# A residual add moved from VectorE to an accumulating DMA in a seven-product Strassen-like cross network kernel

## The chip, the cores and the metric

The kernel runs on one core of one Trainium2 chip. The metric is device time in microseconds (us); most executions agree within 0.3%. TensorE is called PE below, VectorE DVE, ScalarE ACT, GpSimd POOL, and SyncE (which issues most DMAs here) SP.

## The reference, cut to what matters

```python
# x0: [16384, 1024] bf16, ws: [6, 1024, 1024] bf16, bs: [6, 1024] bf16
x = x0
for l in range(6):
    proj = einsum('bd,de->be', x, ws[l]) + bs[l]
    x = x0 * proj + x          # the residual add is the "+ x"
return x
```

## The kernel before

The batch is cut into 16 pairs of 2 x 512 rows. For each pair the transposed input `x0T` and the running `x` (`xst`) lie in SBUF. The 1024 x 1024 product of a layer is done with seven products of half size instead of eight (Strassen-Winograd): each is 16 matmuls of 128x128 on 128x512. `xst` has four blocks, named (eh, n): eh is the half of the features, n the half of the rows. T1 to T4 are differences of blocks, made on DVE, and are inputs of products. The order of the products is 1, 5, 3, 2, 6, 7, 4. Cuts are marked with `# ...`.

```python
rhs_of = {1: blk(xsrc, 0, 0), 2: blk(xsrc, 1, 0), 3: blk(xsrc, 1, 1), 4: Ts[4][:],
          5: Ts[1][:], 6: Ts[2][:], 7: Ts[3][:]}
# T1 = B(0,1) - B(0,0);  T2 = B(1,1) - T1;  T3 = B(1,1) - B(0,1);  T4 = B(1,0) - T2

def final(Cb, eh, n):
    c = Cb[:, :, n, :]
    nc.vector.tensor_tensor(out=c, in0=c, in1=blk(x0T, eh, n), op=MULT)        # L214
    # ... (last layer of the last pair cut)
    nc.vector.tensor_tensor(out=blk(xst, eh, n), in0=c, in1=blk(xsrc, eh, n), op=ADD)   # L223

product(1, pA, True);  P1s = evac(pA)
product(5, pX, True);  P5s = evac(pX)
product(3, pX, False); S53 = evac(pX, bias_eh=0)
product(2, pX2, True); P2s = evac(pX2, bias_eh=0)
nc.vector.tensor_tensor(out=C1[:, :, 0, :], in0=P1s, in1=P2s, op=ADD);  final(C1, 0, 0)
product(6, pA, False)
# ... U2s + S53
final(C1, 0, 1)
# T1 of the next layer
product(7, pA, False)
# ... U3s + P5s
final(C2, 1, 1)
product(4, pA, False)
# ...
final(C2, 1, 0)
# T2, T3, T4 of the next layer
```

Two more things share the DMA engines. Every product loads its own 512 KB of weights, about nine products ahead, all issued in order by SP. At the turn from one pair to the next, SP also issues a transpose of the finished `xst`, two stores of 1 MB, and two transposing loads of the next `x0`.

```python
            if l == (2 if pr == 0 else 0) and not last_pair:
                x0T_next = x0t_pool.tile([P, 2, KD, NB], BF16, name="x0T")
                for n in range(2):
                    ti = nc.sync.dma_start_transpose(out=x0T_next[:, n], in_=x0[...])   # L268
```

Of the kernel before, what the change touches and what calls it, by code (L numbers as in the profile page):

```python
# [7 lines left out]
ADD = mybir.AluOpType.add  # L8
SUB = mybir.AluOpType.subtract
MULT = mybir.AluOpType.mult  # L10
BF16 = mybir.dt.bfloat16
# [5 lines left out]
def kernel(  # L17
# [7 lines left out]
    nc = tc.nc  # L25
    P = nc.NUM_PARTITIONS
# [3 lines left out]
    KH = KD // 2  # L30
    H = D // 2
    NB = 512
# [11 lines left out]
    cb_pool = ctx.enter_context(tc.tile_pool(name="cbp", bufs=2))  # L44
# [29 lines left out]
    def prefetch_upto(n):  # L74
        while state["next"] < min(n, len(all_keys)):
            k_ = all_keys[state["next"]]
            if is_dma(k_) and k_ not in wtiles:
                wt = wring.tile([P, KH, H], BF16, name="wp")
                state["last_dma"] = nc.sync.dma_start(wt[:], w_src(k_[1], k_[2]))
                wtiles[k_] = wt  # L80
            state["next"] += 1

    def blk(t, dh, n):
        return t[:, n, dh * KH:(dh + 1) * KH, :]
# [28 lines left out]
    def load_w12(l):  # L113
        st = combo_st.setdefault(l, {})
        if "w12" not in st:
            st["w12"] = w12_pool.tile([P, KH, H], BF16, name="w12")
            state["last_dma"] = nc.sync.dma_start(st["w12"][:], ws[l][0:H, H:D].rearrange("(k p) e -> p k e", p=P))
        return st["w12"]
# [40 lines left out]
    for pr in range(NPAIR):  # L159
        x0T = x0T_next  # L160
        xst = xst_pool.tile([P, 2, KD, NB], BF16, name="xst")
# [3 lines left out]
        def out_region(eh, n):  # L165
            if xo_last["t"] is None:
                xo_last["t"] = xo_pool.tile([P, 2, 2, KH, KH, P], BF16, name="xoS")
            ti = nc.sync.dma_start_transpose(out=xo_last["t"][:, eh, n].rearrange("p j k r -> p (j k) r"),
                                             in_=xo_last["xfin"][:, eh, n].rearrange("r j k p -> r (j k p)"))
            xo_last["regions"].append((eh, n))  # L170
            xo_last["tins"] = xo_last.get("tins", []) + [ti]
        for l in range(L):
            xsrc = x0T if l == 0 else xst
            Ts = Tn["T"]
            Tn = {"T": {}, "do": ()}
            rhs_of = {1: blk(xsrc, 0, 0), 2: blk(xsrc, 1, 0), 3: blk(xsrc, 1, 1), 4: Ts[4][:], 5: Ts[1][:], 6: Ts[2][:], 7: Ts[3][:]}
            bias_col = lambda eh, m: b_all[:, l * KD + eh * KH + m: l * KD + eh * KH + m + 1]
            if pr == 0 and l + 1 < L:
                prefetch_upto(key_pos[(0, l + 1, 4)] + 1)
                load_w12(l + 1)  # L180
            flush_saves()
            pA = [psA.tile([P, 2, NB], FP32, name="pa") for _ in range(2)]
            C1 = cb_pool.tile([P, KH, 2, NB], BF16, name="cb")
            C2 = cb_pool.tile([P, KH, 2, NB], BF16, name="cb")
            nxt_src = xst if l + 1 < L else None
            combos_next = pr == 0 and l + 1 < L

            def product(pid, pts, start):
                key = (pr, l, pid)
                prefetch_upto(key_pos[key] + PREF)  # L190
                wt = wtiles.pop(key) if not (pr == 0 and pid in (1, 2, 4)) else wtiles[key]
                rhs = rhs_of[pid]
                for m in range(KH):
                    for k in range(KH):
                        kw = {} if start else dict(skip_group_check=True)
                        nc.tensor.matmul(pts[m // 2][:, m % 2, :], lhsT=wt[:, k, m * P:(m + 1) * P], rhs=rhs[:, k, :],  # L196
                                         start=(start and k == 0), stop=(k == KH - 1), **kw)

            def evac(pts, bias_eh=None, dst=None):
                if dst is None:  # L200
                    e = ev_pool.tile([P, KH, NB], BF16, name="ev")
                    dst = e[:]
                if bias_eh is None:
                    for h in range(2):
                        nc.scalar.copy(out=dst[:, 2 * h:2 * h + 2, :], in_=pts[h][:])  # L205
                else:
                    for m in range(KH):
                        nc.scalar.activation(out=dst[:, m, :], in_=pts[m // 2][:, m % 2, :], func=IDENT,  # L208
                                             bias=bias_col(bias_eh, m), scale=1.0)
                return dst  # L210

            def final(Cb, eh, n):
                c = Cb[:, :, n, :]
                nc.vector.tensor_tensor(out=c, in0=c, in1=blk(x0T, eh, n), op=MULT)  # L214
                if last_pair and l == L - 1:
                    if xo_last["xfin"] is None:
                        xo_last["xfin"] = xst_pool.tile([P, 2, 2, KH, KH, P], BF16, name="xst")
                    v4 = lambda a: a.rearrange("r k (j p) -> r k j p", p=P)
                    nc.vector.tensor_tensor(out=xo_last["xfin"][:, eh, n].rearrange("r j k p -> r k j p"),  # L219
                                            in0=v4(c), in1=v4(blk(xsrc, eh, n)), op=ADD)  # L220
                    out_region(eh, n)
                else:
                    nc.vector.tensor_tensor(out=blk(xst, eh, n), in0=c, in1=blk(xsrc, eh, n), op=ADD)  # L223

            product(1, pA, True)
            P1s = evac(pA)
            pX = [psX.tile([P, 2, NB], FP32, name="px") for _ in range(2)]
            product(5, pX, True)
            P5s = evac(pX)
            product(3, pX, False)  # L230
            S53 = evac(pX, bias_eh=0)
            pX2 = [psX.tile([P, 2, NB], FP32, name="px") for _ in range(2)]
            product(2, pX2, True)
            P2s = evac(pX2, bias_eh=0)
            nc.vector.tensor_tensor(out=C1[:, :, 0, :], in0=P1s, in1=P2s, op=ADD)  # L235
            final(C1, 0, 0)
            if combos_next:
                emit_combo(l + 1, 5)
            product(6, pA, False)
            U2s = evac(pA)  # L240
            nc.vector.tensor_tensor(out=C1[:, :, 1, :], in0=U2s, in1=S53, op=ADD)  # L241
            final(C1, 0, 1)
            if nxt_src is not None:
                Tn["do"] = (1,)
                emit_T(nxt_src, Tn)
            if combos_next:
                emit_combo(l + 1, 6)
            product(7, pA, False)
            U3s = evac(pA, bias_eh=1)
            nc.vector.tensor_tensor(out=C2[:, :, 1, :], in0=U3s, in1=P5s, op=ADD)  # L250
            final(C2, 1, 1)
            if combos_next:
                emit_combo(l + 1, 3)
            product(4, pA, False)
            evac(pA, bias_eh=1, dst=C2[:, :, 0, :])
            final(C2, 1, 0)
            if nxt_src is not None:
                Tn["do"] = (2, 3, 4)
                emit_T(nxt_src, Tn)
            if combos_next:  # L260
                emit_combo(l + 1, 7)
                if l + 1 == L - 1:
                    stage_ctx.close()
                    xo_pool = ctx.enter_context(tc.tile_pool(name="xo", bufs=1))
# [3 lines that stand above are left out]
                    ti = nc.sync.dma_start_transpose(out=x0T_next[:, n], in_=x0[(pr + 1) * PR + n * NB:(pr + 1) * PR + (n + 1) * NB, :])  # L268
                    if state.get("last_dma") is not None:
                        tc.add_manual_dep(ti.ins, state["last_dma"].ins.name,  # L270
                                          mybir.DependencyInfo(mybir.DependencyClass.NoSync, mybir.DependencyReason.DATA),
                                          reason="keep the x0 prefetch behind the already issued weight loads")
            if l == L - 1 and not last_pair:
                Tn["do"] = (1, 2, 3, 4)
                emit_T(x0T_next, Tn)
# [47 lines left out]
```

## Time and profile before

| | before |
|---|---|
| time, median of 2 runs | 2353.77 us (2353.34 to 2354.19) |
| PE busy | 2312.4 us, 98% of the span |
| DVE busy | 1708.6 us, 73% |
| the 316 residual adds that the change replaces | 385.0 us of DVE, 1222 ns each |

From the page of the kernel before: the engines' busy times, the chain of waits that ended last, the group of the residual add (count, then busy us and mean ns of one, then idle time before it) and two kinds of DMA (count, KB, median us from issue to landing; for transposes no size).

```profile
span 2352.8 us, 27562 instructions
...
PE 2312.4 (98%) x10537; PEld 1052.7 (45%) x10752; DVE 1708.6 (73%) x1464; ACT 1556.7 (66%) x2113; POOL 1.2 (0%) x5
...
PE 96%; DVE 1%; DMA 1%; issue 1%; SPq 1%; ACT 0%; another core or an unknown queue 0%; DVEq 0%
...
L223 DVE TENSOR_TENSOR xst<-cb,xst 128x2048 bf16<-128x2048 bf16 x316 | 385.0, 1222 | 14.5
...
wp<-Lc SPq DMA_DIRECT2D x360, 512.0 KB, 3.4
...
x0T<-in_x_dram SPq DMA_TRANSPOSE x32, 7.3
```

The chain is PE from end to end, so nothing that DVE does is paid for, as long as it is done in time. How much time there is shows in the timeline of one change of layer (start in us, duration, engine, line, operation). Product 6 of the old layer ended near 1000 us.

```profile
1003.38 1.23 DVE L214 TENSOR_TENSOR cb<-cb,x0T 128x2048 bf16<-128x2048 bf16 x1
1004.64 1.22 DVE L223 TENSOR_TENSOR xst<-cb,xst 128x2048 bf16<-128x2048 bf16 x1
...
1006.92 1.22 DVE L93 TENSOR_TENSOR T_7568<-xst 128x2048 bf16<-128x2048 bf16 x1
1007.25 3.62 PE L196 MATMUL pa<-xst,wp 128*128 128x512 bf16 x15
...
1010.71 3.62 PE L196 MATMUL px<-T_7568,wp 128*128 128x512 bf16 x16
...
1014.16 7.07 PE L196 MATMUL px<-xst,wp 128*128 128x512 bf16 x31
```

These are the multiply and the add of block (0,1), then T1, then products 1, 5, and 3 with 2 of the next layer. A product starts every 3.45 us, and no line has a wait. Three products lie between the end of product 6 and product 5 of the next layer, which needs T1. The add is finished 3.6 us before T1 has to start (1010.71 - 1.22 - 1005.86), so the way from the multiply to T1 has some slack, but not much.

The third thing to read is how full the DMA engines are. The windows view gives, for one layer with the transposing loads of `x0` in it and one plain layer, the busy time of each engine, the granted PE clock, the DMA share (1.00 is all 16 engines) and GB/s:

```profile
1055.90:1080.00 24.10, 24.00 (x112) 10.86 (x113) 17.43 (x16) 16.13 (x23) 0.00 (x0) 1.00 1.08 253
1104.30:1128.40 24.10, 23.94 (x111) 10.90 (x112) 17.50 (x16) 16.13 (x23) 0.00 (x0) 1.00 0.45 153
```

A plain layer leaves half the DMA time free; the layer after the turn leaves none.

### The profile page before, as it was taken

What the parts mean: (1) busy time and instruction counts of PE and PEld (TensorE: products, weight loads), DVE (VectorE), ACT (ScalarE), POOL (GpSimd) and SP (SyncE); (2) the same over time, 40 slices, a digit from 0 to 9 for tenths busy, and PEclk for the clock granted to TensorE, in tenths of its full rate; (3) what the DMA queues carried; (4) which work ended last, traced back from release to release, by engine and by line L of the source; (5) the groups of instructions that cost most, each with busy time, mean ns of one, the idle gap of its engine ahead of it and who ended that gap; (6) DMA issues with size and microseconds to landing.
All of it is one profiled execution on the core that took longest, in us unless ns stands there. A gap on an engine that the chain in (4) does not pass through costs nothing.

```text
span 2352.8 us, 27562 instructions
## 1 busy us (share of the span) xinstructions
PE 2312.4 (98%) x10537; PEld 1052.7 (45%) x10752; DVE 1708.6 (73%) x1464; ACT 1556.7 (66%) x2113; POOL 1.2 (0%) x5
## 2 busy tenths in 40 slices
PE   7999999999999999999999999999999999999997
PEld 3444444444444444444444444444444444444443
DVE  5977767676777767676776767677776767777675
ACT  4666666666666666666666666666666666666665
POOL 0000000000000000000000000000000000000000
PEclk9999999999999999999999999999999999999998
DMA  7769485584956849568494774947749476594843
GB/s 226 203 210 256 152 216 196 161 253 154 228 184 171 241 154 240 171 177 235 153 259 153 178 233 152 259 152 190 221 152 260 153 198 214 155 257 152 226 153 86
DMA packets 599987, 457.96 MB, mean 195 GB/s; under 512 B 398128, under 2 KB 550704, under 8 KB 599856
## 3 DMA queue, kind: packets, MB, share of 16 engines
q1 hardware_dynamic: 599856, 456.20, 67.0%
q8 instruction: 85, 1.39, 0.2%
q14 instruction: 46, 0.38, 0.1%
HBM read 342.88 MB, written 46.14 MB: 165 GB/s over the span
## 4 chain that ended last, share of the span: by engine, by line
PE 96%; DVE 1%; DMA 1%; issue 1%; SPq 1%; ACT 0%; another core or an unknown queue 0%; DVEq 0%
PE pa L196 54%; PE px L196 42%; SPq L145 1%; DMA w_313<-in_ws_dram 0%; DMA wp<-in_ws_dram 0%; DVE cb L214 0%; DVE xst L219 0%; DVE xst L223 0%; ACT ev L208 0%; DVE cb L241 0%; DVE cb L250 0%; DVE cb L235 0%; DVE wp L128 0%; DVE T_247 L93 0%; DVE T_811 L93 0%
## 5 line engine op out<-in xcount | busy, mean ns | idle before, releaser
L196 PEld LDWEIGHTS <-wp 128*128 128x128 bf16 x10752 | 1052.7, 98 | 1283.8 <-issue 12.7
L208 ACT ACTIVATE ev<-px,b_all 128x512 bf16<-128x512 f32 x768 | 486.3, 684 | 201.3 <-PE px L196 193.3
L196 PE MATMUL px<-xst,wp 128*128 128x512 bf16 x2510 | 562.5, 379 | 2.7
L235 DVE TENSOR_TENSOR cb<-ev 128x2048 bf16<-128x2048 bf16 x96 | 117.6, 1225 | 594.2 <-ACT ev L208 594.2
L205 ACT CAST ev<-pa 128x1024 bf16<-128x1024 f32 x384 | 388.6, 1012 | 240.2 <-PE pa L196 230.8
L214 DVE TENSOR_TENSOR cb<-cb,x0T 128x2048 bf16<-128x2048 bf16 x384 | 467.8, 1221 | 6.3
L223 DVE TENSOR_TENSOR xst<-cb,xst 128x2048 bf16<-128x2048 bf16 x316 | 385.0, 1222 | 14.5
L208 ACT ACTIVATE ev<-pa,b_all 128x512 bf16<-128x512 f32 x384 | 243.1, 684 | 112.9 <-PE pa L196 108.2
L208 ACT ACTIVATE cb<-pa,b_all 128x512 bf16<-128x512 f32 x384 | 243.1, 684 | 88.4 <-ACT ev L208 48.4
L196 PE MATMUL pa<-xst,wp 128*128 128x512 bf16 x1254 | 287.3, 379 | 1.3
L205 ACT CAST ev<-px 128x1024 bf16<-128x1024 f32 x192 | 194.3, 1012 | 138.1 <-PE px L196 133.1
L241 DVE TENSOR_TENSOR cb<-ev 128x2048 bf16<-128x2048 bf16 x96 | 117.0, 1219 | 0.0
L250 DVE TENSOR_TENSOR cb<-ev 128x2048 bf16<-128x2048 bf16 x96 | 117.0, 1218 | 0.0
L196 PE MATMUL px<-x0T,wp 128*128 128x512 bf16 x501 | 112.4, 379 | 0.5
L223 DVE TENSOR_TENSOR xst<-cb,x0T 128x2048 bf16<-128x2048 bf16 x64 | 78.3, 1223 | 1.5
L196 PE MATMUL pa<-x0T,wp 128*128 128x512 bf16 x251 | 60.2, 391 | 12.9 <-DMA x0T<-in_x_dram 12.6
L130 DVE TENSOR_TENSOR wp<-wp 128x2048 bf16<-128x2048 bf16 x6 | 7.3, 1219 | 2.1 <-DMA wp<-in_ws_dram 2.1
L128 DVE TENSOR_TENSOR wp<-wp 128x2048 bf16<-128x2048 bf16 x6 | 7.3, 1219 | 0.0
L126 DVE TENSOR_TENSOR wp<-w_90,wp 128x2048 bf16<-128x2048 bf16 x1 | 1.2, 1226 | 8.2 <-DMA wp<-in_ws_dram 8.2
L93 DVE TENSOR_TENSOR T_111<-x0T 128x2048 bf16<-128x2048 bf16 x1 | 1.2, 1226 | 5.7 <-DMA x0T<-in_x_dram 5.7
L219 DVE TENSOR_TENSOR xst<-cb,xst 128x2048 bf16<-128x2048 bf16 x4 | 4.9, 1225 | 0.1
L196 PE MATMUL px<-T_247,wp 128*128 128x512 bf16 x16 | 3.6, 378 | 0.3 <-DVE T_247 L93 0.3
(783 smaller groups left out, 1858.9 us busy)
## 6 DMA issues: line engine op xcount, KB each, us to landing
wp<-Lc SPq DMA_DIRECT2D x360, 512.0 KB, 3.4
wp<-in_ws_dram SPq DMA_DIRECT2D x288, 512.0 KB, 3.7
out_dram<-x0T SPq DMA_DIRECT2D x30, 1024.0 KB, 9.8
Lc<-wp SPq DMA_DIRECT2D x24, 512.0 KB, 3.1
out_dram<-xoS SPq DMA_DIRECT2D x4, 512.0 KB, 4.7
w_90<-in_ws_dram SPq DMA_DIRECT2D x1, 512.0 KB, 4.7
x0T<-in_x_dram SPq DMA_TRANSPOSE x32, 7.3
w_130<-in_ws_dram SPq DMA_DIRECT2D x1, 512.0 KB, 5.0
```

The source lines that it names most:

```text
L128: nc.vector.tensor_tensor(out=t_[:], in0=wtiles[(0, l, 5)][:], in1=W11[:], op=SUB)
L130: nc.vector.tensor_tensor(out=t_[:], in0=W21[:], in1=wtiles[(0, l, 6)][:], op=SUB)
L145: nc.sync.dma_start_transpose(out=x0T_next[:, n], in_=x0[n * NB:(n + 1) * NB, :])
L196: nc.tensor.matmul(pts[m // 2][:, m % 2, :], lhsT=wt[:, k, m * P:(m + 1) * P], rhs=rhs[:, k, :], start=(start and k == 0), stop=(k == KH - ...
L205: nc.scalar.copy(out=dst[:, 2 * h:2 * h + 2, :], in_=pts[h][:])
L208: nc.scalar.activation(out=dst[:, m, :], in_=pts[m // 2][:, m % 2, :], func=IDENT, bias=bias_col(bias_eh, m), scale=1.0)
L214: nc.vector.tensor_tensor(out=c, in0=c, in1=blk(x0T, eh, n), op=MULT)
L219: nc.vector.tensor_tensor(out=xo_last["xfin"][:, eh, n].rearrange("r j k p -> r k j p"), in0=v4(c), in1=v4(blk(xsrc, eh, n)), op=ADD)
L223: nc.vector.tensor_tensor(out=blk(xst, eh, n), in0=c, in1=blk(xsrc, eh, n), op=ADD)
L235: nc.vector.tensor_tensor(out=C1[:, :, 0, :], in0=P1s, in1=P2s, op=ADD)
L241: nc.vector.tensor_tensor(out=C1[:, :, 1, :], in0=U2s, in1=S53, op=ADD)
L250: nc.vector.tensor_tensor(out=C2[:, :, 1, :], in0=U3s, in1=P5s, op=ADD)
```

## The change

The intent: DVE is busy 73% of the time, DMA engines have time to spare, and a DMA issued from GpSimd can add to its destination. So from layer 1 on the residual add `x += x0*proj` becomes an accumulating DMA from the product tile into `xst`. The product tile also gets a layout in which each block is contiguous, for 4 KB rows. Layer 0 keeps the DVE add, since its source is `x0T` and not `xst`.

```diff
-            C1 = cb_pool.tile([P, KH, 2, NB], BF16, name="cb")
-            C2 = cb_pool.tile([P, KH, 2, NB], BF16, name="cb")
+            C1 = cb_pool.tile([P, 2, KH, NB], BF16, name="cb")
+            C2 = cb_pool.tile([P, 2, KH, NB], BF16, name="cb")
 ...
-                c = Cb[:, :, n, :]
+                c = Cb[:, n]
 ...
+                elif l > 0:
+                    nc.gpsimd.dma_start(blk(xst, eh, n), c, accum_op=ADD)
                 else:
                     nc.vector.tensor_tensor(out=blk(xst, eh, n), in0=c, in1=blk(xsrc, eh, n), op=ADD)
 ... (four more lines index C1 and C2 in the new layout)
```

## The prediction

> **What bounds the kernel now.** TensorE. The page gives PE 2312.4 us busy of a 2352.8 us span (98%), the chain of waits is 96% PE, and the granted clock is 1.00 in every layer I read. The timeline shows one product of 16 matmuls starting every 3.45 us and a layer of seven products every 24.17 us. VectorE is busy 1708.6 us (73%), but the waits view shows PE waiting for it only 0.3 us twice.
>
> **Removed.** 316 VectorE adds (group xst<-cb,xst, 1222 ns each): 386 us of VectorE time, none of it on the chain.
>
> **Added.** 316 accumulating DMAs of 512 KB, SBUF to SBUF, issued by GpSimd. Packets of 4096 bytes take 159 ns here, so a plain 512 KB copy keeps each engine busy 8 x 159 ns = 1.27 us. The Trainium skill ("Collectives: The Full Stack", "The bandwidth ceiling") says that a reduce in the DMA needs two source reads and runs at half the copy rate: estimate 2.5 us of data. The fixed part is about 2 us ("DMA: Bandwidth & Descriptors", "Anatomy of one DMA", and the weight loads agree: 3.4 us to landing for 1.3 to 1.6 us of data). Weight loads share the engines, one per 3.45 us (DMA share 0.47 in plain layers, 1.08 in the layer with the x0 transposes). Estimate from the end of the multiply to landing: D = 6.5 us in plain layers, 5 at best, 8 to 10 where transposes and a backlog of weight loads are in the queue. An add took 1.2 us.
>
> **What lies on the critical path.** I read the slack from the timeline at 1000 to 1018 us, times from the end of product 6 (about 1000):
> - (0,0): multiply ends 1000.9, product 1 of the next layer starts 1007.25. Stall if D > 6.4.
> - (0,1): its multiply can end at 4.05; T1 takes 1.22 and product 5 starts at 10.7. Stall D - 5.4.
> - (1,0): VectorE is in order and T1 precedes this multiply, so T1's wait for the DMA holds it. It ends at 6.5 + D and lands at 6.5 + 2D; product 2 was due at 17.6. The accumulated stall is 2D - 11.1.
> - (1,1): never binding.
>
> These stalls recur at 4 layer ends per pair (layers 1 to 4) x 16 pairs = 64. D = 5.5 costs nothing; 6.5 gives 1.9 us x 64 = 122 us; 8 gives 314 us. A gain is nearly impossible.
>
> **Predicted time.** 2490 us, range 2352 to 2760. Faster by over 2%: 0.01; within 2%: 0.24; slower: 0.75.
>
> **What the profile would show.**
> - VectorE busy falls by about 386 us to about 1320 us, with more idle time, ended by the DMA xst<-cb before T1.
> - PE idle appears before product 5 (px<-T1) and product 2 (px<-xst), waiting for VectorE T1 and the DMA; l = 1 is worst.
> - A software queue of 316 DMAs, 166 MB written, median D of 5 to 8 us; DMA share of plain layers rises from 0.47 to about 0.9.
> - Products still start every 3.45 us between stalls; layer 0 of each pair keeps 24.17 us.
>
> **What would make it wrong.** If descriptor generation on GpSimd for a two-source DMA is slow, or the adder in the DMA runs well below half the copy rate, D reaches 10 us and the loss 500 us or more. If contention is milder and D stays under 5.5 us, the time is the same. If a backlog of weight loads starves PE, stalls show on wp, not on xst.

## The result, and the profile after

The changed kernel takes 2753.44 us (median of 2 runs, 2748.07 to 2758.80), against 2353.77 us: 400 us more. The ratio is 1.1698 (95% interval 1.1644 to 1.1753). Ratios here are the mean time of one kernel's runs over that of the other's runs of the same rounds, so not quite the ratio of the medians quoted. The result is correct. The direction was predicted, and the time lies just inside the range, but the loss is three times the 136 us forecast.

The same parts of the page, after:

```profile
span 2746.2 us, 28149 instructions
...
PE 2415.0 (88%) x10752; PEld 1064.7 (39%) x10752; DVE 1369.6 (50%) x1148; ACT 1555.5 (57%) x2113; POOL 273.0 (10%) x321
...
q1 hardware_dynamic: 599856, 456.20, 58.1%
q0 software_dynamic: 45504, 165.70, 33.3%
...
PE 12%; DMA 6%; DVE 2%; ACT 1%; issue 1%; POOL 0%; DVEq 0%; POOLq 0%; ACTq 0%
...
wp<-Lc SPq DMA_DIRECT2D x360, 512.0 KB, 6.4
xst<-cb POOLq DMA_DIRECT2D x316, 512.0 KB, 7.6
...
x0T<-in_x_dram SPq DMA_TRANSPOSE x32, 11.5
```

DVE lost its work (1708.6 to 1369.6 us). The new queue q0 moves 165.70 MB. The accumulating DMA takes 7.6 us from issue to landing where the add took 1.2, and everything else in the DMA queues takes longer too: a weight load 6.4 us instead of 3.4, an `x0` transpose 11.5 instead of 7.3. (The chain of waits accounts for too little of this span to be read.)

**A plain change of layer.** The timeline, for the same steps as shown of before; in brackets the idle time of the engine before the line, and what ended it:

```profile
1164.63 1.22 DVE L214 TENSOR_TENSOR cb<-cb,x0T 128x2048 bf16<-128x2048 bf16 x1
...
1166.15 0.86 POOL L223 DMA_DIRECT2D xst<-cb  x1 [2.11 <-DVE cb L214]
...
1169.03 3.62 PE L196 MATMUL pa<-xst,wp 128*128 128x512 bf16 x16
...
1173.37 1.23 DVE L93 TENSOR_TENSOR T_7387<-xst 128x2048 bf16<-128x2048 bf16 x1 [3.81 <-DMA xst<-cb]
1174.51 1.22 DVE L214 TENSOR_TENSOR cb<-cb,x0T 128x2048 bf16<-128x2048 bf16 x1
1174.65 3.61 PE L196 MATMUL px<-T_7387,wp 128*128 128x512 bf16 x16 [2.00 <-DVE T_7387 L93]
```

The multiply of (0,1) ends at 1165.85 (1164.63 + 1.22), T1 can start at 1173.37: 7.5 us, and product 5 waits 2.0 us. Note the line at 1174.51: the multiply of block (1,0) runs behind T1, although the last ACT operation on its tile had ended at 1170.49.

**The crowded change of layer**, from layer 1 to 2 of a pair, where the `x0` transposes are in the queue:

```profile
1092.44 14.06 SPq L270 DMA_TRANSPOSE x0T<-in_x_dram  x2
...
1099.15 1.23 DVE L214 TENSOR_TENSOR cb<-cb,x0T 128x2048 bf16<-128x2048 bf16 x1
...
1100.67 0.87 POOL L223 DMA_DIRECT2D xst<-cb  x1 [2.09 <-DVE cb L214]
...
1115.98 1.23 DVE L93 TENSOR_TENSOR T_7025<-xst 128x2048 bf16<-128x2048 bf16 x1 [11.90 <-DMA xst<-cb]
...
1117.26 6.35 PE L196 MATMUL px<-T_7025,wp 128*128 128x512 bf16 x16 [9.43 <-DVE T_7025 L93]
```

Here the same step took 15.6 us (1115.98 - 1100.38), product 5 waited 9.4 us, and then its 16 matmuls took 6.35 us instead of 3.6, because the clock had fallen: the trace's clock records show half clock for 10.2 us, from 5.4 us after the gap began.

**Where the 393.4 us of the profiled spans went.** In every trace all 10752 weight loads of PE are recorded. From their start times one gets the idle gap before each product (last weight load of one product to the second of the next, less two matmul pitches of 0.216 us). Summed over the run, in us; the kernel before has 0.9 us in all:

| entry into layer | before product 1 | 5 | 3 | 2 | sum | per entry (16) |
|---|---|---|---|---|---|---|
| 2 | 33.0 | 91.7 | 0.6 | 21.9 | 147.2 | 9.2 |
| 3 | 24.7 | 47.2 | 0.9 | 12.9 | 85.7 | 5.4 |
| 4 | 1.8 | 38.8 | 2.4 | 1.8 | 44.7 | 2.8 |
| 5 | 2.5 | 41.7 | 0.8 | 0.0 | 45.0 | 2.8 |
| all | 62.0 | 219.4 | 4.7 | 36.6 | 322.6 | |

The total with 0.5 us elsewhere is 323 us, 322 more than before. The other 71 us (393.4 - 322) are matmuls at a lower clock. In the trace every one of the 24 products that started after a gap of over 3.5 us was slow (over 1 us longer than 3.45), 12 of the 40 after a gap of 2 to 3.5 us, and of the 608 after a smaller gap only the very first. The Trainium skill says why ("TensorE: Matmul & The Clock Gate", "What's actually happening"): PE falls to half clock after an idle window of about 3.4 us and needs about as much work to come back. The trace agrees in that the recorded clock is 1 or one half and nothing else, and that 22 of its 37 half-clock stretches last 3.4 us and 8 last 6.8. The length of the gap alone does not decide, though: here gaps from 2.2 us on could be enough, and in `e_x0split_t1late`, an experiment below, 7 of the 15 products after gaps of over 3.5 us ran at full clock, the longest of these gaps being 3.84 us.

**What the time of the DMA is made of.** From the records of the DMA packets one can tell when the first packet of each accumulating DMA started and the last ended. D is from the end of the multiply to the end of the last packet; T1, the reader, started another 0.4 to 0.5 us later in the last three runs of the table (layer 4) and 0.6 to 0.8 us later in the change (medians). Medians for block (0,1), pairs 1 to 14:

| run, layer | multiply to issue | issue to first packet | first to last packet | D |
|---|---|---|---|---|
| change, layer 4 | 0.30 | 3.10 | 4.13 | 7.50 |
| change, layer 1 | 0.30 | 6.13 | 5.36 | 10.49 (mean 13.17) |
| `e_copy` (no adding), layer 4 | 0.30 | 2.69 | 1.96 | 4.96 |
| `e_noload` (no weight loads), layer 4 | 0.30 | 1.43 | 2.77 | 4.49 |
| `e_01only` (no other block by DMA), layer 4 | 0.29 | 1.86 | 3.36 | 5.46 |

The last three are experiments below.

What the DMA of (0,1) waits for in a plain layer is not what one might think. In layers 3 and 4 of pairs 1 to 14 its first packet starts, in 25 of 28 cases, 0.5 to 1.6 us after the last packet of (0,0) has ended, and in between the packets of a weight load take 69 to 98% of the engines' time. That weight load is itself held up by (0,0): its first packet comes 1.8 us after its issue and its last 5.0 us, against 1.0 and 3.1 us in the kernel before and 1.1 and 3.0 us in `e_01only` (medians). So in a plain layer the DMAs of the two queues take turns almost as wholes. Without weight loads (`e_noload`) the DMA of (0,0) is there too, and (0,1) doesn't wait for it: 1.43 us from issue to first packet, the same as for (0,0).

### The profile page after: what moved, and what is told of

Same layout as the page of the kernel before. It is cut to its first block, busy times and chain, and to the rows that moved or that the text cites. A ratio compares the mean times of both kernels' runs of the same rounds, so it can differ in the third digit from the quotient of the medians.

```text
span 2746.2 us, 28149 instructions
## 1 busy us (share of the span) xinstructions
PE 2415.0 (88%) x10752; PEld 1064.7 (39%) x10752; DVE 1369.6 (50%) x1148; ACT 1555.5 (57%) x2113; POOL 273.0 (10%) x321
## 3 DMA queue, kind: packets, MB, share of 16 engines
q0 software_dynamic: 45504, 165.70, 33.3%
## 5 line engine op out<-in xcount | busy, mean ns | idle before, releaser
L196 PEld LDWEIGHTS <-wp 128*128 128x128 bf16 x10752 | 1064.7, 99 | 1664.8 <-issue 453.5
L196 PE MATMUL px<-xst,wp 128*128 128x512 bf16 x2560 | 575.9, 382 | 36.1 <-DMA xst<-cb 30.7
L223 POOL DMA_DIRECT2D xst<-cb x316 | 271.9, 860 | 2422.2 <-DVE cb L214 1199.9
L196 PE MATMUL pa<-xst,wp 128*128 128x512 bf16 x1280 | 303.5, 392 | 56.7 <-DMA xst<-cb 56.5
L196 PE MATMUL px<-T_621,wp 128*128 128x512 bf16 x16 | 6.5, 594 | 23.0 <-DVE T_621 L93 23.0
L196 PE MATMUL px<-T_10304,wp 128*128 128x512 bf16 x16 | 5.7, 532 | 17.0 <-DVE T_10304 L93 17.0
L196 PE MATMUL px<-T_3746,wp 128*128 128x512 bf16 x16 | 6.3, 578 | 13.2 <-DVE T_3746 L93 13.2
L196 PE MATMUL px<-T_7025,wp 128*128 128x512 bf16 x16 | 6.4, 586 | 9.4 <-DVE T_7025 L93 9.4
## 6 DMA issues: line engine op xcount, KB each, us to landing
out_dram<-x0T SPq DMA_DIRECT2D x30, 1024.0 KB, 10.2
x0T<-in_x_dram SPq DMA_TRANSPOSE x32, 11.5
```

What stands on the lines that cost most here:

```text
L196: nc.tensor.matmul(pts[m // 2][:, m % 2, :], lhsT=wt[:, k, m * P:(m + 1) * P], rhs=rhs[:, k, :], start=(start and k == 0), stop=(k == KH - ...
L223: nc.gpsimd.dma_start(blk(xst, eh, n), c, accum_op=ADD)
```

## The experiments

The theory after reading the traces (**L**, latency): the loss is the time from the multiply to the landing where it exceeds the slack of the reader, plus the slow clock after each long gap. Parts of it: **Q**, the two-source read makes the data part long, and the DMAs of the queue wait for each other; **S**, sharing the engines with weight loads; **X**, the collision with the `x0` transposes at the entry of layer 2; **V**, the wait for a DMA on in-order DVE holds the operations behind it. The main rival (**C**, contention): the extra DMA traffic itself starves the weight loads, or GpSimd's work slows DVE. Seventeen kernels ran, each against the kernel before on the same chip (its median was 2353.75 to 2354.45 us each time); "gaps" are the sums as in the table above. Three kernels had one or two executions over 1.5% above their fastest, marked slow; ratios use the fast ones, and for `e_scr4` and `e_t1force` these are only two of four. The times given are medians of all four.

### e_layout: the layout alone

```diff
-                elif l > 0:
-                    nc.gpsimd.dma_start(blk(xst, eh, n), c, accum_op=ADD)
```

> Only the layout of the product tile changes, the add stays on VectorE. Both theories: the same as before, 2354 us within 0.3%, adds still 1.22 us each. If the layout costs anything, it shows here.

2354.04 us, ratio 1.000 (0.9985 to 1.0015). The layout costs and gives nothing.

### e_l5only: accumulate only where no product waits

```diff
-                elif l > 0:
+                elif l == L - 1:
```

> Accumulating DMAs only in layer 5, where no product waits for the result, VectorE adds in layers 1 to 4. Theory L (the latency on the way to the next layer's products costs): 2354 to 2370 us, no gap before products 1, 5, 2 of layers 2 to 5; the later output transpose may cost a little at layers 0 to 2 of the next pair. Rival (every accumulating DMA costs about 400/316 = 1.3 us wherever it is): 60 x 1.3 = 76 us, 2430 us.

2354.60 us, ratio 1.0003 (0.9988 to 1.0018), gaps 0.9 us.

```profile
PE 2312.0 (98%) x10537; PEld 1052.5 (45%) x10752; DVE 1641.4 (70%) x1404; ACT 1555.5 (66%) x2113; POOL 52.9 (2%) x65
...
xst<-cb POOLq DMA_DIRECT2D x60, 512.0 KB, 7.8
```

Sixty accumulating DMAs with a median landing time of 7.8 us, as long as in the change, are free when the reader is far away. And 60 adds fewer on DVE gain nothing. A fixed price per DMA is ruled out.

### e_copy and e_noload: what makes the DMA slow

Their outputs are wrong, which doesn't matter for the times.

```diff
-                    nc.gpsimd.dma_start(blk(xst, eh, n), c, accum_op=ADD)
+                    nc.gpsimd.dma_start(blk(xst, eh, n), c)                        # e_copy
```

> Wrong result on purpose: the DMA copies instead of accumulating, so each destination is not read. Theory Q (the two-source read makes the data part 2.9 us instead of 1.3 us, and that length also makes the next DMA queue): packets about 160 ns instead of 328 ns, D of block (0,1) in plain layers from 7.5 us to 4.5 to 5 us, no stall before product 5 in plain layers, total 2354 to 2450 us, what is left lying at the entry of layer 2. Rival F (the fixed cost of a GpSimd DMA dominates): D above 6.5 us and over 2600 us.

```diff
+                if k_[0] > 0:
+                    wtiles[k_] = wfix        # e_noload: one resident tile from pair 1 on
+                else:
                     wt = wring.tile([P, KH, H], BF16, name="wp")
                     state["last_dma"] = nc.sync.dma_start(wt[:], w_src(k_[1], k_[2]))
```

> Wrong result on purpose: from the second pair on no weight is loaded, every product uses one resident tile; accumulating DMAs as in the change. Theory S (sharing the 16 engines with weight loads adds 1 to 1.5 us to D): D of (0,1) in plain layers from 7.5 to about 5.5 to 6 us, gaps at the entry of layers 4 and 5 fall from 2.8 us to under 1 us, total 2370 to 2480 us. Rival: the accumulating DMAs only wait for each other and for their own fixed cost, D stays above 7 us and the entry gaps stay 2.5 us or more, total over 2600 us.

`e_copy`: 2448.71 us, ratio 1.0405 (1.0390 to 1.0421); gaps 81.5 us, of which 62.6 at the entry of layer 2. Its packets of 4096 bytes take 159 ns (median), those of the accumulating DMA 328 ns. The Trainium skill ("Collectives: The Full Stack", "The bandwidth ceiling: the fold count and why AG ≠ RS ≠ AR") says that a reduce in the DMA reads two sources, and so runs at half the rate of a copy. The page says it of a collective operation; the packets here agree with the rate (328 / 159 = 2.06), and no run shows that the second read is the reason. `e_noload`: 2399.79 us, ratio 1.0189 (1.0172 to 1.0206), gaps 39.0 us. From the pages of `e_copy` and of `e_noload`, in this order:

```profile
xst<-cb POOLq DMA_DIRECT2D x316, 512.0 KB, 4.4
...
xst<-cb POOLq DMA_DIRECT2D x316, 512.0 KB, 4.5
```

Each run takes away one of two things and nearly all of the loss goes: 305 of 400 us and 354 of 400. That is no contradiction. D of (0,1) falls from 7.5 to 5.0 and to 4.5 us; with 0.5 us to the reader that is 5.5 and 5.0 against a slack of 5.4 us. Near or below the slack, a DMA costs little or nothing (gaps before product 5 at the entries of layers 4 and 5: 4.9 and 7.6 us for 32 entries, against 80.5 in the change). Both the length of the packets (Q) and the weight loads (S) matter, and their effects must not be added. But the part of Q by which the DMAs of one queue wait for each other is not seen without weight loads.

### e_x0split, e_t1late, e_x0split_t1late: two repairs of the change

```diff
# e_x0split: one x0 transpose in layer 2, one in layer 3, after product 7's weights
-            if l == (2 if pr == 0 else 0) and not last_pair:
+            if l in (2, 3) and not last_pair:
+                if l == 2:
                     x0T_next = x0t_pool.tile([P, 2, KD, NB], BF16, name="x0T")
-                for n in range(2):
+                for n in (l - 2,):
```

```diff
# e_t1late: T1 emitted after the multiply of (1,0)
-            if nxt_src is not None:
-                Tn["do"] = (1,)
-                emit_T(nxt_src, Tn)
...
-                Tn["do"] = (2, 3, 4)
+                Tn["do"] = (1, 2, 3, 4)
```

> As the change, but the two transposing loads of the next pair's x0 are issued apart, one in layer 2 and one in layer 3, just after product 7's weights, instead of both at the end of layer 0. Theory X (the stall at the entry of layer 2, 193 us of the 400 with the slow clock after it, is there because layer 1's accumulating DMAs queue behind these transposes and the weight loads held up by them): the entry of layer 2 falls to the size of the later ones, 40 to 60 us in all, total 2590 to 2640 us. Rival: the entry of layer 2 is bad for another reason (the output transposes and stores of layer 0): little changes, over 2700 us.

> As the change, but T1 is issued on VectorE after the multiply of block (1,0), so the wait for the DMA of (0,1) no longer holds that multiply. Theory V (the in-order VectorE costs the gaps before product 2, 37 us, and lets the DMA of (1,0) start late): gaps before product 2 under 10 us, those before product 5 unchanged or a little larger because the DMAs queue closer, total 2690 to 2730 us. Rival: the (1,0) DMA now competes with that of (1,1) and the total stays within 10 us of the change.

> Both repairs together. If they act on different gaps they add: 2540 to 2610 us. What is left is the plain latency before product 5 (2 to 3 us at each of 64 entries).

`e_x0split`: 2625.72 us, ratio 1.116 (1.1119 to 1.1200). The gaps at the entry of layer 2 fell from 147 to 88 us and those of layer 3 from 86 to 49, the size of layers 4 and 5. So X holds for about 130 us of the 400. The total is in the range expected; the entry of layer 2 isn't, which was to fall to 40 to 60 us. But before product 1 of layer 2 the gap grew, from 33 to 53 us: there the accumulating DMA of (0,0) still queues, 4.5 us from issue to first packet against 1.7 us in layer 2. In the packet records of one pair, weight loads fill the engines until it starts; that they are catching up after the output transpose and stores, which SP issues just before, is the likely reason, but not tested.

`e_t1late`: 2736.42 us, ratio 1.1633 (1.1576 to 1.1691), not clear of the change; both together 2646.20 us, ratio 1.122 (1.1166 to 1.1273), no better than `e_x0split` alone. The order of DVE in the built kernel explains it: the scheduler, which orders each engine's instructions when a kernel is built, had put T1 ahead of the (1,0) multiply again. V was not tested by these two.

### e_traffic, e_traffic_x0split, e_scr4: the traffic without the latency

The DVE add stays, and the same accumulating DMAs go into scratch tiles that nobody reads.

```diff
+    scr = [const.tile([P, KH, NB], BF16, name=f"scr{i}") for i in range(2)]   # e_scr4: range(4)
...
                     nc.vector.tensor_tensor(out=blk(xst, eh, n), in0=c, in1=blk(xsrc, eh, n), op=ADD)
+                    if l > 0:
+                        nc.gpsimd.dma_start(scr[n][:], c, accum_op=ADD)       # e_scr4: scr[2 * eh + n]
```

> The VectorE add stays, and the same 316 accumulating DMAs go into a scratch tile that nobody reads. Theory L (what costs is the latency from the multiply to the landing, on the way to the next layer's products): 2354 to 2370 us, PE without gaps. Rival C (what costs is the extra DMA traffic itself: weight loads starve, or GpSimd's descriptor writing slows VectorE): 2500 us or more, with PE waiting for wp or VectorE operations longer than 1.22 us.

> The scratch-traffic kernel with the x0 transposes apart. If the 77 us of the traffic kernel are weight loads held up in the pile of transposes, stores and accumulating DMAs of layers 0 and 1, most of it goes: 2354 to 2385 us. If the traffic costs everywhere, it stays at 2430 us.

> As e_traffic, with four scratch tiles instead of two, so that no scratch DMA waits for the one before and no product tile is held for long. Theory L (traffic alone is nearly free, the latency is what costs): 2354 to 2390 us. Rival C (traffic alone costs, by starved weight loads in the crowded layers): 2420 us or more, with PE waiting for wp.

`e_traffic` took 2430.77 us (ratio 1.0328, 1.0295 to 1.0362) and `e_traffic_x0split` 2691.10 us (1.1389, 1.1316 to 1.1462). They are flawed as tests: with two scratch tiles each DMA waits for an earlier one (POOL waited 760 and 1133 us for it), holds its product tile meanwhile, and in the second kernel DVE then waited for product tiles (277 us). `e_scr4`, with four scratch tiles, is the cleaner one: POOL waits 3.2 us for a scratch DMA in all, and ACT and DVE 31 us for product tiles that such DMAs still hold. It took 2511.51 us (median of four runs between 2480 and 2595; ratio of the two fast ones 1.0566, 1.0526 to 1.0606). So theory L alone falls: the traffic by itself costs over 120 us in this kernel. Its gaps, 124 us, lie elsewhere than in the change: 89 us before product 2 of layer 2, nearly all in six of the sixteen pairs, and 27 us once in the first pair (there the two `x0` transposes took 42.1 us of SP's time against 12.6 before, and DVE, on which PE waited, had waited 20 us for weights). One of the six in the timeline, after the same transposes in one pair of the kernel before (first line):

```profile
1063.11 10.86 SPq L268 DMA_TRANSPOSE x0T<-in_x_dram  x2
...
1717.88 24.19 SPq L293 DMA_TRANSPOSE x0T<-xst  x1
...
1756.48 27.05 SPq L273 DMA_TRANSPOSE x0T<-in_x_dram  x2
...
1770.79 3.62 PE L199 MATMUL px<-xst,wp 128*128 128x512 bf16 x16
1792.15 5.37 PE L199 MATMUL px<-xst,wp 128*128 128x512 bf16 x16 [17.74 <-DMA wp<-in_ws_dram]
```

And from the waits view of the same run (who waited for what, us in total, times, longest):

```profile
PEld L199 <- DMA wp<-in_ws_dram: 96.3, 10, 23.4
PE px L199 <- DMA wp<-in_ws_dram: 87.7, 8, 22.9
```

The two `x0` transposes, 9 to 11 us of SP's time per pair in the kernel before, took 27 us here, where four accumulating DMAs fell on them. In the packet records the accumulating packets have nearly all of the engines' time from 1764 to 1770 us (the 256-byte packets, which are the transposes' here, 1 to 6%), and 78 to 86% from 1770 to 1776 us, with 26 to 29% for the transposes (records can overlap, so sums pass 100%). The weight loads stand behind the transposes in SP's queue, and PE waits 17.7 us for weights. In the change PE waits for weights hardly at all (8.9 us of weight-load waits in the whole run): its own stalls, I think, give the loads time. The other half of the rival falls: DVE is busy 1708 us in these runs as in the kernel before, so GpSimd's work does not slow it. So there is a second limit beside the latency. It can't be carried over to the change as a number: with scratch tiles nothing makes the transpose of the finished `xst` wait for the accumulating DMAs of layer 5, and it took 13.5 to 24.2 us of SP's time (24.19 in the pair shown), against 9.5 to 10.4 in the kernel before and in the change. Why six pairs were hit and ten were not was not followed up.

### e_01only and e_no01: one block, and all but that one

```diff
-                elif l > 0:
+                elif l > 0 and (eh, n) == (0, 1):     # e_01only;  e_no01: != (0, 1)
```

> Only block (0,1) is accumulated by DMA in layers 1 to 5, the other three by VectorE. Theory Q (about 1.5 us of the 8 us of D(0,1) is queueing behind the DMA of (0,0) on the same queue): from issue to first packet 1.4 us instead of 3.1, D to the last packet 5 to 6.3 us, so with 5.4 us of slack the gap before product 5 in plain layers is 0.3 to 1.5 us per entry instead of 2.6; total 2370 to 2440 us. Rival (no queueing, D is what one such DMA takes): D 7.5 us, 2.6 us per entry, total over 2480 us.

> The reverse: (0,1), the block with the least slack, goes back to VectorE, the other three stay DMAs. Theory L (slack decides): no gap before product 5 at the entries of layers 3 to 5, and before products 1, 3 and 2 there under 10 us in all, although three quarters of the traffic remain; at the entry of layer 2, 40 to 100 us remain before products 1 and 2. Total 2380 to 2480 us. Rival (loss goes with the number of DMAs): 0.75 x 400 = 300 us, 2650 us.

`e_01only`: 2538.05 us, ratio 1.078 (1.0762 to 1.0798). In plain layers nearly as expected: 1.9 us from issue to first packet instead of 3.1 (1.4 was expected), D 5.5 us, gaps of 1.2 us per entry instead of 2.8. The total missed because the entry of layer 2 kept 84.8 us of gaps, D 9.9 us there.

`e_no01`: 2729.20 us, ratio 1.1595 (1.1565 to 1.1625), although the block with the least slack was back on DVE. A clear miss. The gaps before product 5 were gone, but 45 to 49 us at each entry of layers 3 to 5 (77 at layer 2) had appeared before product 3, which reads (1,1). The timeline shows why:

```profile
1174.92 1.23 DVE L93 TENSOR_TENSOR T<-xst 128x2048 bf16<-128x2048 bf16 x1 [1.65 <-DMA xst<-cb]
...
1176.06 1.22 DVE L252 TENSOR_TENSOR cb<-ev 128x2048 bf16<-128x2048 bf16 x1
1177.31 2.36 DVE L214 TENSOR_TENSOR cb<-cb,x0T 128x2048 bf16<-128x2048 bf16 x2
...
1179.07 0.86 POOL L223 DMA_DIRECT2D xst<-cb  x1 [8.87 <-PE pa L196]
...
1185.19 8.51 PE L196 MATMUL px<-xst,wp 128*128 128x512 bf16 x32 [2.94 <-DMA xst<-cb]
```

The scheduler put T1 ahead of the sum and multiply of (1,1). T1 waits for the DMA of (0,0), and DVE, which works in order, keeps the (1,1) block waiting too; its DMA is issued late and product 3 waits 2.9 us.

### e_t1force and e_no01force: the order of DVE, forced

```diff
-                nc.vector.tensor_tensor(out=t_[:], in0=B12, in1=B11, op=SUB)
+                t1i = nc.vector.tensor_tensor(out=t_[:], in0=B12, in1=B11, op=SUB)
+                if which.get("late"):       # order only, no semaphore
+                    tc.add_manual_dep(t1i.ins, state["mult"].ins.name, NoSync, ...)
# e_t1force: behind the (1,0) multiply;  e_no01force: e_no01, behind the (1,1) multiply
```

> The edit of e_t1late left the built order as it was (T1 still ahead of the multiply of (1,0)); here a dependency forces T1 behind it. Theory V (VectorE in order: T1's wait for the DMA of (0,1) holds that multiply): the gaps before product 2 (37 us in the change) fall under 12 us, those before product 5 stay, so the total falls by 10 to 40 us to 2710 to 2745 us. Rival (the order of VectorE has no part in it): gaps before product 2 stay over 30 us.

> As e_no01, with T1 forced behind the multiply of (1,1). Theory V says the 2.9 us per entry before product 3 in e_no01 came from T1, which waits for the DMA of (0,0), holding that multiply (estimate: multiply ends 10.9 + 6.3 to landing = 17.2 against 14.2): they fall under 0.5 us per entry in layers 3 to 5, and those three entries hold under 30 us of gaps together instead of 158; total 2450 to 2530 us. Rival (loss follows the number of DMAs): stays over 2680 us.

`e_t1force`: 2675.73 us, ratio 1.1275 (1.1183 to 1.1366). The gaps before product 2 are gone (36.6 to 0.7 us), as V says. The total fell by more than expected; the gaps at the entries of layers 2 and 3 also fell (147 to 100, 86 to 59), and 20 us came in at layer 1, where T1 now waits for the last multiply. The total differs between executions of this kernel by nearly as much (2636 to 2684 us), and only one was profiled, so I don't put the rest down to the order.

`e_no01force`: 2554.53 us, ratio 1.084 (1.0796 to 1.0884), 175 us less than `e_no01` by the order of DVE alone. The gaps before product 3 fell to 2.4 us in layers 3 to 5. The total is 25 us above the range expected, and the entries of layers 3 to 5 kept 91 us of gaps instead of under 30. Of these, 41 us lie before product 1 of layer 3, where the DMA of (0,0) in layer 2 took 4.0 us to its first packet while weight loads filled the engines (in the one pair looked at). The other 45 us lie before product 2, up to 23 us per layer, where the (1,0) DMA comes after that of (1,1) (4.0 us from issue to first packet).

### e_mix, e_mixforce, e_11force: how much can be moved for nothing

```diff
-                elif l > 0:
+                elif l > 0 and eh == 1:     # e_mix, e_mixforce;  e_11force: (eh, n) == (1, 1)
# all three with the x0 transposes apart;
# e_mix with T1 as in e_t1late, the others with T1 forced behind the (1,1) multiply
```

> Accumulating DMA only for the two blocks of the second half, (1,1) and (1,0), T1 after the multiply, the x0 transposes apart. Theory L: 2354 to 2380 us, the same as before, with 160 VectorE adds fewer and no gain, because VectorE is not what bounds. Rival (freed VectorE time gives something back): under 2345 us.

> Accumulating DMA for (1,1) and (1,0) alone, x0 transposes apart, T1 forced behind the multiply of (1,1) and ahead of that of (1,0). Estimate from e_mix: (1,1) is multiplied by 8.1 us and lands at 14.3 against 14.2; (1,0) is multiplied by 10.6 and lands at 17.7 against 17.6. So gaps of 0 to 0.3 us per entry instead of 1.8 to 2.6, total 2355 to 2390 us against 2504. Rival: 2480 us or more.

> Accumulating DMA for (1,1) alone, nothing queued before it, T1 behind its multiply, x0 transposes apart. From e_mixforce: the (1,1) multiply ends about 8.1 us after product 6, D to landing 5.1 + 0.5 us, product 3 starts at 14.2. Theory L (only a DMA that lands after its reader was due costs): gaps under 0.3 us per entry, total 2354 to 2368 us with 79 DMAs in flight. Rival (each such DMA costs about 1.2 us wherever it is): 2440 us or more.

| run | time | ratio (95%) | gaps | before product 3 | before product 2 |
|---|---|---|---|---|---|
| e_mix | 2504.19 | 1.0641 (1.0625 to 1.0657) | 145.6 | 85.8 | 51.9 |
| e_mixforce | 2447.17 | 1.0385 (1.0365 to 1.0405) | 90.6 | 23.0 | 65.3 |
| e_11force | 2369.77 | 1.0064 (1.0048 to 1.0081) | 15.2 | 13.1 | 0.0 |

Both expectations for the mixed kernels were too low, by 124 and 57 us. In `e_mix` the scheduler had once more put T1 ahead of a multiply, here that of (1,1), which then starts about 1.0 us later than in `e_mixforce` (in the entry looked at); forcing T1 behind it took the gaps before product 3 from 85.8 to 23.0 us. And I had again left out that the (1,0) DMA comes after that of (1,1) and a weight load (5.0 us from issue to first packet in `e_mix`, 3.7 in `e_mixforce`, 1.4 for the first of the two). With (1,1) alone nothing is ahead of it, D is 5.2 us, and 79 accumulating DMAs cost 16 us, just above the range expected and by the 95% interval under 1%. It gains nothing: no version beat the kernel before, because DVE time was never paid for.

## Why the prediction was wrong

The step that failed is the sum of the stalls, "6.5 gives 1.9 us x 64 = 122 us": it took one D, that of a plain layer, for all 64 layer ends. The 32 entries of layers 2 and 3, near the turn of the pair, lost 233 us where the sum has 61; there the mean D of (0,1) in layer 1 was 13.2 us. The other 32 lost 90 us where it has 61, because D was 7.3 to 7.5 us and not 6.5. And the matmuls at a lower clock, 71 us, have no term in it. Together that is 272 us more than the sum. The mechanism, a DMA that lands after T1 has to start, was right. Point by point:

- **PE bounds, DVE time is not paid for: right.** `e_layout` and `e_l5only` (60 adds fewer) show the same time. DVE fell by 339 us where I wrote 386: back-to-back operations overlap a little (79 us in all in the records of the kernel before, 34 us after), so 316 times 1222 ns was too much.
- **The accumulating DMA delays T1 and so product 5: right, and the largest part** (219 of 323 us of gaps).
- **The data part of 2.5 us by the rate of two reads: the size was right.** Eight packets of 328 ns are 2.6 us, and 2.77 us were measured without weight loads. The fixed part of "about 2 us" was right as well: 1.43 us to the first packet, 0.3 before and 0.5 after (`e_noload`).
- **D = 6.5 us in plain layers: too small.** Measured: 7.5 us to the last packet (layer 4), and 8.0 and 8.5 to the reader (layers 3 and 4). Without weight loads it is 4.5 and 5.0 us. With the weight loads but no other block by DMA it is 5.5; with the other blocks by DMA too, another 2.0 us come on top, 1.2 of them before the first packet, while a weight load that (0,0) had held up has the engines. My sum had the weight loads in it, but not that one accumulating DMA delays the next through them. The slack of 5.4 us holds: 8.0 and 8.5 less 5.4 is 2.6 and 3.1, and the entries of layers 4 and 5 lost 2.8 us each.
- **The accumulated stall of 2D - 11.1: wrong, and by luck small.** It used one D for all blocks. With D = 8.0 it gives 4.9 us, but in plain layers the (1,0) DMA has nothing ahead of it and takes 5.0 us to its last packet (1.43 us to the first). DVE does hold the (1,0) multiply (`e_t1force`), for 37 us in all.
- **(0,0) stalls product 1 if D > 6.4: right as a rule.** In layers 3 and 4 its D was 5.5 us and product 1 lost 4.3 us in 32 entries; in layers 1 and 2 the mean D was 8.0 and 7.2 us and it lost 57.7. The sum has nothing for it.
- **(1,1) never binding: right** in the order that the change was built with (4.7 us before product 3), and wrong in `e_no01`, where the scheduler chose another.
- **All 64 entries taken as plain in the forecast (64 x 1.9 = 122): wrong, and the largest part of the miss.** I had named 8 to 10 us for the layer with the transposes and left it out of the sum. Mean D of (0,1) there was 13.2 us (median 10.5), the entries of layers 2 and 3 lost 233 of the 323 us of gaps, and taking the transposes apart gave 128 us back.
- **The slow clock: not in the sum.** 71 us, after the gaps. No run tests it by itself; that it follows the gaps is what the records show.
- **Smaller forecasts: near.** DMA share of three later layers 0.80 to 0.83 (forecast 0.9), median time from issue to landing 7.6 us (forecast 5 to 8 from the multiply).
- **"Stalls show on wp" if weights starve: it did not show in the change.** In the change PE waited 8.9 us for weights. With the latency taken away and the traffic kept (`e_scr4`) it waits 88 us before matmuls, and the whole costs over 120 us. That the stalls of the change are what gives the loads time is argued, not tested.

What stays open: how much of the collision in layers 1 and 2 is due to the output transpose and stores rather than the `x0` transposes; only the latter were moved. Also open is what the slow clock costs by itself, and the rest of the fall in `e_t1force`.

## What to carry to other kernels

When work moves from an engine to a DMA, compare the time from its input to its reader, not the busy time, and compute it with everything that stands ahead on the DMA engines, in the busiest stretch, not for one DMA alone. An in-order engine that waits for a DMA also delays everything scheduled behind the wait, so look at the built order. Where the engine that was relieved is not what bounds, there is nothing to win that could pay for the risk.

## What the Trainium skill lacked or had wrong

- "DMA: Bandwidth & Descriptors" says that an accumulating DMA must come from GpSimd, but gives no time for one. Here 512 KB from SBUF to SBUF took 7.6 us from issue to landing in the median among weight loads (4.5 in `e_noload`), 328 ns per 4096-byte packet against 159 for a copy.
- The same page ("Queues, rings and completion order") has the engines go round-robin between queues by packets, but doesn't say what that means next to transposes: in `e_scr4` two `x0` transposes took 27 us of SP's time instead of 9 to 11 while accumulating packets had 78 to 86% of the engines' time. A packet of the accumulating DMA takes 328 ns (4096 bytes) and one of the transposes 18 ns (256 bytes); whether the turns between them explain it, no run shows.
- "TensorE: Matmul & The Clock Gate" gives about 3.4 us of idle time before the clock falls. In the change 12 of 40 products after gaps of 2 to 3.5 us were slow as well, the shortest gap being 2.2 us; in `e_x0split_t1late` 7 of 15 after gaps of over 3.5 us were not, the longest of these being 3.84 us.
